# The MLP's turning and the gate moved behind the head loop of a one-token attention and MLP kernel

## The chip, the cores and the metric

The kernel runs on one core of a Trainium2 chip. The metric is the device time of one execution in microseconds. Three timed runs of the kernel before took 135.38, 135.53 and 135.91; the median is 135.53 us. One more execution was taken with the hardware profiler.

## What is computed

One token `x` of 576 features goes through two branches, mixed by a gate that is one number:

```python
g = sigmoid((x * gate_w).sum(-1))                       # gate_w: 576
q = (x @ wq) as 32 heads of 128                          # wq: 576 x 4096
k, v = the last 4096 of 32768 cached rows, 16 heads, each used by 2 query heads
p = softmax(q . k * 128 ** -0.5)
a = (p . v) @ wo                                         # wo: 4096 x 576
b = gelu_tanh(x @ w1 + b1) @ w2 + b2                     # w1: 576 x 4608, w2: 4608 x 576
out = g * a + (1 - g) * b                                # 1 x 576
```

All inputs are bf16. The cached rows in use are 33.6 MB of keys and values; the four weight matrices are 20 MB.

## The kernel before

**Transfers.** Keys and values come in four tiles each (`k_t`, `v_t`, 4 MB, 4 key heads a tile; here k0 to k3 and v0 to v3). They share three buffers of `kv_pool` with two tiles of w2. wq, w1 and wo come in two tiles each through two buffers of `w_pool`. Nearly all are issued by SP, in this order: the first part of wq, k0, `x9` (x as 64 rows of 9), the rest of wq, k1, two pieces of b1, k2, v0, first half of w1, k3, second half of w1, v1, v2, v3, two tiles of wo, and w2 in four groups, of which the last two are cut in pieces (L690). An issue that needs a buffer waits on SP until its last reader is done, and all later issues wait behind it: v0 takes k0's buffer, k3 that of k1, v1 that of k2, v2 that of v0, v3 that of k3, and so on. ScalarE issues five small transfers at the start: b2 in two halves, x as one row of 576 (`x_row`) in two halves, and the gate's weights (`gw_row`).

**Head of the program.** Constants are made on VectorE and GpSimd. Then x is spread over 128 partitions: TensorE makes `x_ps` from `x9` (L428) and four VectorE operations write `x2` (L436), which every product with wq and w1 uses as its stationary side. Then the gate: VectorE multiplies and sums `x_row` and `gw_row` (`junk`, `s0`, L440), TensorE spreads the sum to all partitions (`g_ps`, L445), ScalarE takes Exp (`ge`, L447), and VectorE makes `g_t` = g and `omg` = 1 - g (L448 to L452). Then come the transposes of the first four head units (L456), the query product (`q_ps`, L465), its turning (`qT`, `qz`) and the scores of three units.

**Transposes and scores.** A key tile is worked off in four units h (16 units in all). `transposes(h, i)`, i from 0 to 7, turns four 128 x 128 blocks by matmuls into one of three PSUM buffers (L281) and evicts them into `kT`, by VectorE for i = 0, 3, 6 (L290) and by ScalarE else (L292). `scores(h, s)` multiplies `kT` by the query (L311) into one PSUM tile for half of the units: units 0 to 7 are the first half, 8 to 15 the second.

**The head loop** (L618) goes over h from 3 to 15: it makes the transposes of unit h + 1, the scores of unit h, and between them, one function at a time, whatever stands in three lists. `chain` is the softmax of the first half (from h = 8): `row_max`, `turn_max`, `spread` (ScalarE's long Exp, L355) and four `put`, which turn the probabilities into `ez` (L366, L373). `tail` takes out the first value tile's sums. `mlp` is the MLP's middle, filled behind h = 13 once both halves of w1 are multiplied (`w1_mul`, L509): `take` adds b1 (`h_r`, L528), nine `turn_h` turn the features by two fp32 matmuls each (L539), and `act` makes gelu times `omg` out of them (L550 to L571, the result `gt`). Two of them are called for each i > 1, so they stand between the transposes of unit 15 in h = 14 and behind them. The first value tile's products (`values`, L397) run in h = 10 and 11.

**Behind the loop** (L659) `row_max`, `turn_max` and `spread` of the second half stand between the units of the second value tile (`unit(4)` to `unit(7)`); then `take` of `heads_out(1)` (`a_s`, L409 and L413), the four `put`, `norm`, and the units of the third and fourth value tiles. Then `ot`, `ow` (L696 to L712), the products with wo and three groups of w2 into `part` (L734), b2's part (`part_s`, L742), the last group of w2 in quarters into `y_ps` (L753), four copies into `y` (L769) and the output's transfer.

Each engine works off its instructions in the order of this text, since the order is written by hand (`manual_schedule`). One PSUM buffer (`ps_m`, one tag) serves all small products in turn: `x_ps`, `g_ps`, `qT`, `hT`, `mT`, `mb`, `pT`, `o_ps`, `t_ps`, `ow_ps`.

Of the kernel before, what the change touches and what calls it, by code (L numbers as in the profile page):

```python
# [8 lines left out]
FP32 = mybir.dt.float32  # L9
BF16 = mybir.dt.bfloat16  # L10
ACT = mybir.ActivationFunctionType
ALU = mybir.AluOpType
# [4 lines left out]
def kernel(  # L17
# [94 lines left out]
    def load_k(m):  # L112
        return load_kv(A_k_cache, m, "k_t")
# [14 lines left out]

    k_tiles, v_tiles = {}, {}

    x_row = const.tile([1, D], BF16, name="x_row")
    gw_row = const.tile([1, D], BF16, name="gw_row")

    b2_r = const.tile([P, D], BF16, name="b2_r")
    nc.gpsimd.memset(b2_r[:], 0.0)

    for o in (slice(0, D // 2), slice(D // 2, D)):
        nc.scalar.dma_start(out=b2_r[0:1, o], in_=B_b2.rearrange("(o n) -> o n", o=1)[:, o])
    for o in (slice(0, D // 2), slice(D // 2, D)):
        nc.scalar.dma_start(out=x_row[:, o], in_=A_x.rearrange("a b d -> (a b) d")[:, o])  # L140
    nc.scalar.dma_start(out=gw_row[:], in_=gate_w.rearrange("(o n) -> o n", o=1))

    x9 = const.tile([P // 2, NM], BF16, name="x9")

# [15 lines left out]
    for o in range(2):  # L160
        nc.sync.dma_start(
            out=b1_r[o : o + 32 * (NQ - 1) + 1 : 32],
            in_=B_b1.rearrange("(o t k n) -> o t k n", o=2, t=NQ, k=2)[o],
        )
    k_tiles[2] = load_k(2)


# [108 lines left out]
    def transposes(h, i):  # L276
        if i == 0:
            kT[h] = kT_pool.tile([P, W], BF16, name="kT", tag="kT")
        tp = ps_t.tile([P, BC * P], FP32, name="tp", tag="tp")
        for c in range(BC):  # L280
            nc.tensor.matmul(  # L281
                tp[:, c * P : (c + 1) * P],
                lhsT=k_tiles[h // UT][:, (h % UT) * NCH + i * BC + c, :],
                rhs=perm[:],
                start=True,
                stop=True,
            )
        dst = kT[h][:, i * BC * P : (i + 1) * BC * P]
        if i in (0, 3, 6):
            nc.vector.tensor_copy(out=dst, in_=tp[:])  # L290
        else:
            nc.scalar.copy(out=dst, in_=tp[:])  # L292
# [131 lines left out]

    x_ps = ps_m.tile([P, NM], FP32, name="x_ps", tag="m")
    nc.tensor.matmul(x_ps[:], lhsT=dup[:], rhs=x9[:], start=True, stop=True)  # L428
    ev, od = par[:, 0:1], par[:, 1:2]
    for dst, src, s in (  # L430
# [4 lines left out]
    ):  # L435
        nc.vector.tensor_scalar(out=dst, in0=src, scalar1=s, scalar2=None, op0=ALU.mult)  # L436

    junk = const.tile([1, D], BF16, name="junk")
    s0 = const.tile([1, 1], FP32, name="s0")
    nc.vector.tensor_tensor_reduce(  # L440
        out=junk[:], in0=x_row[:], in1=gw_row[:], scale=1.0, scalar=0.0,
        op0=ALU.mult, op1=ALU.add, accum_out=s0[:],
    )
    g_ps = ps_m.tile([P, 1], FP32, name="g_ps", tag="m")
    nc.tensor.matmul(g_ps[:], lhsT=ones_ff[0:1, :], rhs=s0[:], start=True, stop=True)  # L445
    ge = const.tile([P, 1], FP32, name="ge")
    nc.scalar.activation(out=ge[:], in_=g_ps[:], func=ACT.Exp, scale=-1.0)  # L447
    nc.vector.tensor_scalar(out=ge[:], in0=ge[:], scalar1=1.0, scalar2=None, op0=ALU.add)  # L448
    g_t = const.tile([P, 1], FP32, name="g_t")
    nc.vector.reciprocal(out=g_t[:], in_=ge[:])  # L450
    omg = const.tile([P, 1], FP32, name="omg")
    nc.vector.tensor_scalar(  # L452
        out=omg[:], in0=g_t[:], scalar1=-1.0, scalar2=1.0, op0=ALU.mult, op1=ALU.add
    )

    for h in range(UT):  # L456
        for i in range(NBL):
            transposes(h, i)
    v_tiles[0] = load_v(0)
# [59 lines left out]
    def gelu():  # L519

        NF = RJ * NG
        C0 = 0.7978845608028654
        h_r = small.tile([P, 2, 2, FB], FP32, name="h_r", tag="big")
        box = []

        def take():
            for k in range(2):
                nc.vector.tensor_tensor(  # L528
                    out=h_r[:, :, k, :],
                    in0=h_box[0][:, k : k + 1, 0:FB].to_broadcast([P, 2, FB]),  # L530
                    in1=b1_r[:, k : k + 1, :].to_broadcast([P, 2, FB]),
                    op=ALU.add,
                )
            box.append(ps_m.tile([P, RJ, 2, NG], FP32, name="hT", tag="m"))

        def turn_h(j):

            rows = h_r[:].rearrange("p e k n -> p (e k n)")
            nc.tensor.matmul(  # L539
                box[0][:, j, :, :].rearrange("p e g -> p (e g)"),  # L540
                lhsT=rows[:, j : j + RJ * (P - 1) + 1 : RJ],
                rhs=sel_f[:].rearrange("p e g -> p (e g)"),
                start=True,
                stop=True,
            )

        def act():
            hacc = const.tile([P, NF], FP32, name="hacc")
            h_v = hacc[:].rearrange("p (j g) -> p j g", j=RJ)
            nc.vector.tensor_scalar(  # L550
                out=h_v, in0=box[0][:, :, 0, :], scalar1=half[:, 0:1], scalar2=None, op0=ALU.mult
            )
            nc.vector.scalar_tensor_tensor(
                out=h_v, in0=box[0][:, :, 1, :], scalar=half[:, 1:2], in1=h_v, op0=ALU.mult,
                op1=ALU.add,
            )
            z2 = const.tile([P, NF], FP32, name="z2")
            nc.vector.tensor_tensor(out=z2[:], in0=hacc[:], in1=hacc[:], op=ALU.mult)
            poly = const.tile([P, NF], FP32, name="poly")
            nc.vector.tensor_scalar(  # L560
                out=poly[:], in0=z2[:], scalar1=2.0 * C0 * 0.044715, scalar2=2.0 * C0,
                op0=ALU.mult, op1=ALU.add,
            )
            u_t = const.tile([P, NF], FP32, name="u_t")
            nc.vector.tensor_tensor(out=u_t[:], in0=poly[:], in1=hacc[:], op=ALU.mult)
            e_t = const.tile([P, NF], FP32, name="e_t")
            nc.scalar.activation(out=e_t[:], in_=u_t[:], func=ACT.Exp, scale=-1.0)
            nc.vector.tensor_scalar(out=e_t[:], in0=e_t[:], scalar1=1.0, scalar2=None, op0=ALU.add)
            r_t = const.tile([P, NF], FP32, name="r_t")
            nc.vector.reciprocal(out=r_t[:], in_=e_t[:])  # L570
            nc.vector.scalar_tensor_tensor(  # L571
                out=gt[:].rearrange("p j g -> p (j g)"), in0=hacc[:], scalar=omg[:, 0:1], in1=r_t[:],
                op0=ALU.mult, op1=ALU.mult,
            )

        return [take] + [lambda j=j: turn_h(j) for j in range(RJ)] + [act]
# [37 lines left out]
        for s in range(2):  # L614
            scores(h, s)

    chain, tail, mlp = [], [], []
    for h in range(UT - 1, NU):  # L618
        if h == 2 * UT - 1:
            k_tiles[3] = load_k(3)  # L620
            w1_t.append(w1_load(1))
        if h == 3 * UT - 1:
            v_tiles[1] = load_v(1)
        for i in range(NBL):
            if h < NU - 1:
                transposes(h + 1, i)
            at = (4, 6) if h % (TB * UT) == 0 else (2, 5)
            if i in at:
                scores(h, at.index(i))
            if i in (0, 1, 3, 6, 7) and chain:  # L630
                chain.pop(0)()
            if i in (0, 5) and tail:
                tail.pop(0)()
            if i > 1 and mlp:
                for f in mlp[:2]:
                    f()
                mlp = mlp[2:]
            if h in (10, 11) and i % 2 == 1:
                for j in range(4):
                    n = (h - 10) * 16 + (i - 1) * 2 + j  # L640
                    values(n // NBL, n % NBL)
        if h == 11:
            tail = heads_out(0)
            w1_mul(0, w1_t[0])
        if h == 13:
            w1_mul(1, w1_t[1])
            mlp = gelu()
        if h == TB * UT - 1:
            chain = softmax(0)
    v_tiles[2] = load_v(2)  # L650
# [4 lines left out]
    def unit(h):  # L655
        for i in range(NBL):
            values(h, i)

    row_max()  # L659
    unit(UT)  # L660
    turn_max()
    unit(UT + 1)
    spread()
    unit(UT + 2)
    unit(UT + 3)
    take, turn_out = heads_out(1)
    take()
# [18 lines left out]
    for g in range(NG):  # L686
        if g % 3 == 0:
            t = kv_pool.tile([P, NCK * Dh], BF16, name="w2_t", tag="kv")
        at = (g % 3) * RJ * D
        cut = {NG - 2: (0, 5 * D), NG - 1: (0, 6 * D, 8 * D, RJ * D - DQ)}.get(g, (0,))  # L690
        for lo, hi in zip(cut, (*cut[1:], RJ * D)):
            nc.sync.dma_start(out=t[:, at + lo : at + hi], in_=w2_view[g, :, lo:hi])
        w2_t.append(t[:, at : at + RJ * D])
# [71 lines left out]

    y = const.tile([1, D], BF16, name="y")
    for t in range(NQ):
        copy = nc.scalar.copy if t < 2 else nc.vector.tensor_copy
        copy(out=y[:, quarters[t]], in_=y_ps[32 * t : 32 * t + 1, :])  # L769
    nc.sync.dma_start(out=out.rearrange("a b n -> (a b) n"), in_=y[:])  # L770

# [29 lines left out]
```

## Time and profile before

| | |
|---|---|
| median of 3 runs | 135.53 us (135.38 to 135.91) |
| the profiled execution's own time | 135.93 us |
| its span, first to last instruction | 134.1 us |
| its mean granted TensorE clock | 0.866 |
| busy: PE, PEld, DVE, ACT, POOL | 91.1, 59.4, 63.3, 50.3, 2.9 us |
| moved by DMA | 53.79 MB, 94.3% of 16 engines' span on SP's queue |
| chain that ended last | DMA 39%, PE 33%, DVE 15%, ACT 5%, issue 4% |

PE is TensorE's matmuls, PEld its weight loads, DVE VectorE, ACT ScalarE, POOL GpSimd. L281 is a line of the kernel. A row of the timeline gives start and busy time in us, engine, line, operation, tiles out and in, partitions by elements, how many were merged, and in brackets the idle time ahead of it and what ended it. The chain that ended last follows the work back from the last instruction. "Issue" is waiting that the profile doesn't explain. The granted clock is 1.0 when TensorE has full speed, 0.5 at half. The times in the text count from the span's start.

### The profile page before, as it was taken

To read this page: it belongs to the slowest core of one execution; us is meant where nothing else is said; L and a number is where in the kernel's file an instruction comes from. 1 tells how busy PE (TensorE), PEld (TensorE's weight loads), DVE (VectorE), ACT (ScalarE), POOL (GpSimd) and SP (SyncE) were. 2 spreads that over 40 slices of the span, in tenths; PEclk is the share of its full clock that TensorE was granted. 3 is DMA by queue.
4 is the path that set the end of the run, shared out by engine and by line. 5 is a ranking of instruction groups with operands and counts; after the bars stand their busy time and mean duration, and the time that the engine had idled before them with its cause. 6 is when DMAs were issued, how large, how long until landed. Compare 5 with 4: busy or idle time off the path is not lost.

```text
span 134.1 us, 2614 instructions
## 1 busy us (share of the span) xinstructions
PE 91.1 (68%) x1127; PEld 59.4 (44%) x1127; DVE 63.3 (47%) x138; ACT 50.3 (37%) x89; POOL 2.9 (2%) x10
## 2 busy tenths in 40 slices
PE   0000299886998885748989989599593585539842
PEld 0000189662666663536555756487122341125420
DVE  2940356673265557555544584624727434450021
ACT  0300057981387777573766467331050000000001
POOL 8000000000000000000000000000000000000000
PEclk9999999999999999995999999965555558965797
DMA  4998999899998998999989999998998999999950
GB/s 115 511 450 350 432 450 489 371 425 472 459 410 376 469 452 355 458 446 469 415 380 458 467 420 401 445 449 362 322 459 357 394 418 440 427 426 413 423 201 6
DMA packets 3431, 53.79 MB, mean 401 GB/s; under 512 B 590, under 2 KB 732, under 8 KB 1372
## 3 DMA queue, kind: packets, MB, share of 16 engines
q1 hardware_dynamic: 3410, 53.62, 94.3%
q8 instruction: 9, 0.15, 0.4%
q14 instruction: 2, 0.02, 0.0%
q10 hardware_dynamic: 10, 0.00, 0.0%
HBM read 53.62 MB, written 0.00 MB: 400 GB/s over the span
## 4 chain that ended last, share of the span: by engine, by line
DMA 39%; PE 33%; DVE 15%; ACT 5%; issue 4%; SPq 1%; DVEq 0%; ACTq 0%
DMA k_t<-in_A_k_cache_dram 16%; PE tp L281 14%; DMA w_t<-in_B_w_dram 14%; DMA x<-in_A_x_dram 9%; PE acc L397 6%; ACT kT L292 5%; DVE kT L290 5%; PE hT L539 3%; PE s_ps L311 2%; DVE ez L373 2%; PE h_ps L509 2%; DVE a_s L413 2%; PE q_ps L465 2%; PE pT L366 1%; DVE h_r L528 1%
## 5 line engine op out<-in xcount | busy, mean ns | idle before, releaser
L292 ACT CAST kT<-tp 128x512 bf16<-128x512 f32 x80 | 44.0, 587 | 30.6 <-PE tp L281 29.7
L281 PE MATMUL tp<-perm,k_t 128*128 128x128 bf16 x512 | 44.8, 234 | 4.3 <-DVE kT L290 2.1
L290 DVE CAST kT<-tp 128x512 bf16<-128x512 f32 x48 | 32.5, 689 | 30.3 <-PE tp L281 28.1
L281 PEld LDWEIGHTS <-k_t 128*128 128x128 bf16 x512 | 35.4, 107 | 15.2 <-issue 12.7
L311 PE MATMUL s_ps<-kT,qz 128*32 128x512 bf16 x128 | 12.8, 415 | 0.4 <-DVE qz L487 0.3
L397 PE MATMUL acc<-v_t,ez 128*32 128x512 bf16 x128 | 12.7, 506 | 0.0
L769 ACT CAST y<-y_ps 1x144 bf16<-1x144 f32 x2 | 0.5, 269 | 30.5 <-PE y_ps L753 30.5
L428 PE MATMUL x_ps<-x,dup 64*128 64x9 bf16 x1 | 0.2, 163 | 14.4 <-DMA x<-in_A_x_dram 14.4
L366 PE MATMUL pT<-pick,pr 128*128 128x128 bf16 x32 | 4.1, 271 | 5.6 <-DVE ez L373 4.2
L373 DVE TENSOR_TENSOR ez<-pT,own_r 128x512 bf16<-128x512 f32 x8 | 5.5, 688 | 4.1 <-PE pT L366 4.1
L366 PEld LDWEIGHTS <-pr 128*128 128x128 bf16 x32 | 2.9, 121 | 7.7 <-issue 5.1
L539 PE MATMUL hT<-sel_f,h_r 128*128 128x8 f32 x18 | 4.9, 378 | 1.4 <-DVE h_r L528 1.4
L355 ACT ACTIVATE pr<-ms,nb 128x2048 bf16<-128x2048 f32 x2 | 4.0, 2002 | 4.9 <-DVE nb L352 4.9
L445 PEld LDWEIGHTS g_ps<-s,ones_ff 1*128 1x128 f32 x2 | 0.5, 308 | 12.1 <-issue 12.1
L539 PEld LDWEIGHTS hT<-sel_f,h_r 128*128 128x128 f32 x18 | 4.7, 332 | 2.1 <-DVE h_r L528 1.7
L311 PEld LDWEIGHTS <-qz 128*32 128x32 bf16 x128 | 3.6, 95 | 4.0 <-issue 1.2
L397 PEld LDWEIGHTS <-ez 128*32 128x32 bf16 x128 | 3.6, 113 | 4.0 <-issue 2.6
L734 PE MATMUL part<-wo_t,ow 128*1 128x288 bf16 x64 | 4.0, 441 | 1.5 <-DVE ow L712 1.5
L447 ACT ACTIVATE ge<-g_ps 128x1 f32<-128x1 f32 x1 | 0.2, 172 | 12.0 <-PE g_ps L445 12.0
L742 DVE SCALAR_TENSOR_TENSOR part_s<-b_r,omg,part 128x576 f32<-128x576 bf16 x1 | 0.8, 814 | 8.2 <-PE part L734 8.2
L420 PE MATMUL o_ps<-m_r,a_s 128*128 128x8 f32 x8 | 1.8, 293 | 4.1 <-DVE a_s L413 3.2
L413 DVE SCALAR_TENSOR_TENSOR a_s<-acc,m_c,a_s 128x128 f32<-128x128 f32 x12 | 4.2, 351 | 0.4
(87 smaller groups left out, 52.8 us busy)
## 6 DMA issues: line engine op xcount, KB each, us to landing
k_t<-in_A_k_cache_dram SPq DMA_DIRECT2D x4, 4096.0 KB, 21.7
v_t<-in_A_v_cache_dram SPq DMA_DIRECT2D x4, 4096.0 KB
w_t<-in_B_w_dram SPq DMA_DIRECT2D x2, 2592.0 KB
wo_t<-in_A_wo_dram SPq DMA_DIRECT2D x2, 2304.0 KB
w_t<-in_B_w_dram SPq DMA_DIRECT2D x2, 1296.0 KB, 24.0
wq_t<-in_A_wq_dram SPq DMA_DIRECT2D x1, 2304.0 KB
wq_t<-in_A_wq_dram SPq DMA_DIRECT2D x1, 1792.0 KB, 14.0
w_t<-in_B_w_dram SPq DMA_DIRECT2D x1, 864.0 KB
```

What stands on the lines that cost most here:

```text
L281: nc.tensor.matmul(tp[:, c * P : (c + 1) * P], lhsT=k_tiles[h // UT][:, (h % UT) * NCH + i * BC + c, :], rhs=perm[:], start=True, stop=True,)
L290: nc.vector.tensor_copy(out=dst, in_=tp[:])
L292: nc.scalar.copy(out=dst, in_=tp[:])
L311: nc.tensor.matmul(s_tiles[t // TB][32 * g : 32 * (g + 1), :, :], lhsT=qz[:, HT * t + g, lo : lo + 32], rhs=kT_v[:, s * CB : (s + 1) * CB, ...
L355: nc.scalar.activation(out=pr[:].rearrange("p c i g -> p (c i) g"), in_=ms[:].rearrange("p c (i g) -> p (c i) g", g=1).to_broadcast([P, CB ...
L366: nc.tensor.matmul(pT[:, c, :, :].rearrange("p x r -> p (x r)"), lhsT=pr[:, n * BC + c, :, :].rearrange("p i g -> p (i g)"), rhs=pick[:].r ...
L373: nc.vector.tensor_tensor(out=ez[:, :, :, n, :, :].rearrange("p t b c r -> p c (t b) r"), in0=pT[:], in1=own_r[:].rearrange("p (a b r) -> ...
L397: nc.tensor.matmul(acc[t][32 * ct : 32 * ct + BC * R, :, :], lhsT=ez[:, t % TB, n // NN, n % NN, :, :].rearrange("p c r -> p (c r)"), rhs= ...
L413: nc.vector.scalar_tensor_tensor(out=a_s[:], in0=acc[t][:, c, :], scalar=m_c[:, c : c + 1], in1=a_s[:], op0=ALU.mult, op1=ALU.add,)
L465: nc.tensor.matmul(q_ps[32 * t : 32 * (t + 1), 0, 0:QC], lhsT=x2[:, m, :], rhs=wq_t[b // QP][:, off : off + QC], start=(m == 0), stop=(m = ...
L539: nc.tensor.matmul(box[0][:, j, :, :].rearrange("p e g -> p (e g)"), lhsT=rows[:, j : j + RJ * (P - 1) + 1 : RJ], rhs=sel_f[:].rearrange(" ...
L734: nc.tensor.matmul(part[32 * t : 32 * t + 1, k, 0:DB], lhsT=col, rhs=w[:, i * D + k * DB : i * D + (k + 1) * DB], start=(n == 0), stop=(n ...
```

## The change

x and the gate's weights are loaded as six rows of 96 each, by SP, between b1 and k2; ScalarE's three transfers for them go. The transposes of unit 0 come ahead of `x_ps` and `x2`. The whole gate (junk to omg) moves from there to behind the head loop, ahead of `row_max`. The MLP's middle leaves the loop: `take` comes behind `row_max`, the nine turnings and `act` behind `unit(6)`. In the last group of w2 the last cut moves from 144 to 288 columns before the end, and the four copies into `y` alternate between ScalarE and VectorE.

```diff
-    x_row = const.tile([1, D], BF16, name="x_row")
-    gw_row = const.tile([1, D], BF16, name="gw_row")
+    GR = 6
+    x_row = const.tile([GR, D // GR], BF16, name="x_row")
+    gw_row = const.tile([GR, D // GR], BF16, name="gw_row")
...
-    for o in (slice(0, D // 2), slice(D // 2, D)):
-        nc.scalar.dma_start(out=x_row[:, o], in_=A_x.rearrange("a b d -> (a b) d")[:, o])
-    nc.scalar.dma_start(out=gw_row[:], in_=gate_w.rearrange("(o n) -> o n", o=1))
...
+    nc.sync.dma_start(out=x_row[:], in_=A_x.rearrange("a b (r n) -> (a b r) n", r=GR))
+    nc.sync.dma_start(out=gw_row[:], in_=gate_w.rearrange("(r n) -> r n", r=GR))
     k_tiles[2] = load_k(2)
...
+    for i in range(NBL):
+        transposes(0, i)
+
     x_ps = ps_m.tile([P, NM], FP32, name="x_ps", tag="m")
...
-    junk = const.tile([1, D], BF16, name="junk")
-    s0 = const.tile([1, 1], FP32, name="s0")
...
-    omg = const.tile([P, 1], FP32, name="omg")
-    nc.vector.tensor_scalar(
-        out=omg[:], in0=g_t[:], scalar1=-1.0, scalar2=1.0, op0=ALU.mult, op1=ALU.add
-    )
-
-    for h in range(UT):
+    for h in range(1, UT):
         for i in range(NBL):
             transposes(h, i)
...
-    chain, tail, mlp = [], [], []
+    chain, tail = [], []
...
-            if i > 1 and mlp:
-                for f in mlp[:2]:
-                    f()
-                mlp = mlp[2:]
...
             w1_mul(1, w1_t[1])
-            mlp = gelu()
...
+    junk = const.tile([GR, D // GR], BF16, name="junk")
+    s0 = const.tile([GR, 1], FP32, name="s0")
+    nc.vector.tensor_tensor_reduce(
+        out=junk[:], in0=x_row[:], in1=gw_row[:], scale=1.0, scalar=0.0,
+        op0=ALU.mult, op1=ALU.add, accum_out=s0[:],
+    )
+    g_ps = ps_m.tile([P, 1], FP32, name="g_ps", tag="m")
+    nc.tensor.matmul(g_ps[:], lhsT=ones_ff[0:GR, :], rhs=s0[:], start=True, stop=True)
+    ge = const.tile([P, 1], FP32, name="ge")
+    nc.scalar.activation(out=ge[:], in_=g_ps[:], func=ACT.Exp, scale=-1.0)
+    nc.vector.tensor_scalar(out=ge[:], in0=ge[:], scalar1=1.0, scalar2=None, op0=ALU.add)
+    g_t = const.tile([P, 1], FP32, name="g_t")
+    nc.vector.reciprocal(out=g_t[:], in_=ge[:])
+    omg = const.tile([P, 1], FP32, name="omg")
+    nc.vector.tensor_scalar(
+        out=omg[:], in0=g_t[:], scalar1=-1.0, scalar2=1.0, op0=ALU.mult, op1=ALU.add
+    )
+
+    take_h, *turns, act = gelu()
     row_max()
+    take_h()
     unit(UT)
     turn_max()
     unit(UT + 1)
     spread()
     unit(UT + 2)
+    for f in turns:
+        f()
+    act()
     unit(UT + 3)
...
-        cut = {NG - 2: (0, 5 * D), NG - 1: (0, 6 * D, 8 * D, RJ * D - DQ)}.get(g, (0,))
+        cut = {NG - 2: (0, 5 * D), NG - 1: (0, 6 * D, 8 * D, RJ * D - DB)}.get(g, (0,))
...
-        copy = nc.scalar.copy if t < 2 else nc.vector.tensor_copy
+        copy = nc.scalar.copy if t % 2 == 0 else nc.vector.tensor_copy
```

More of the change, by code (lines that the diff above doesn't have):

```diff
@@ L436 @@
         nc.vector.tensor_scalar(out=dst, in0=src, scalar1=s, scalar2=None, op0=ALU.mult)
-    junk = const.tile([1, D], BF16, name="junk")
-    s0 = const.tile([1, 1], FP32, name="s0")
-    nc.vector.tensor_tensor_reduce(
-        out=junk[:], in0=x_row[:], in1=gw_row[:], scale=1.0, scalar=0.0,
-        op0=ALU.mult, op1=ALU.add, accum_out=s0[:],
-    )
[L444 to L450, printed above, removed]
-    omg = const.tile([P, 1], FP32, name="omg")
-    nc.vector.tensor_scalar(
-        out=omg[:], in0=g_t[:], scalar1=-1.0, scalar2=1.0, op0=ALU.mult, op1=ALU.add
-    )
-    for h in range(UT):
+    for h in range(1, UT):
         for i in range(NBL):
```

## The prediction

> **What bounds the kernel now.** I read the slices first, then busy time by stage, then SP's waits, then the chain of waits backwards from the end. The transfers are the floor: 53.79 MB go at 430 GB/s from 3 us to 128.5 us, and the row of DMA shares has no hole but a dent near its 28th digit. Busy time by stage (columns: window, its length, busy PE, PEld, DVE, ACT, POOL, granted clock, DMA share, GB/s) sizes that dent:
>
> ```profile
> 60.00:93.00 33.00, 29.55 (x368) 20.98 (x367) 16.53 (x29) 16.19 (x29) 0.00 (x0) 0.87 1.00 430
> 93.00:97.00 4.00, 2.55 (x20) 0.53 (x18) 3.05 (x10) 0.82 (x2) 0.00 (x0) 0.50 0.87 311
> ```
>
> Four microseconds at 311 instead of 430 GB/s lack 0.48 MB, 1.1 us of the stream. The reason is in SP's issues and the timeline:
>
> ```profile
> L104 SPq DMA_DIRECT2D v_t<-in_A_v_cache_dram x4: 534/538/575, 30.1 to 93.3; - x4
> 84.98 1.41 DVE L528 TENSOR_TENSOR h_r<-h_ps,b_r 128x576 f32<-128x576 f32 x2
> 92.68 0.59 PE L281 MATMUL tp<-perm,k_t 128*128 128x128 bf16 x4
> 93.20 1.36 PE L311 MATMUL s_ps<-kT,qz 128*32 128x512 bf16 x8
> 101.91 0.68 DVE L373 TENSOR_TENSOR ez<-pT,own_r 128x512 bf16<-128x512 f32 x1
> ```
>
> v3 is issued at 93.3, when the last transposes of k3 (PE, 92.68) free its buffer. The MLP's turning stands between those transposes (h_r from 84.98), and what was queued before v3 has run out by then. At the end PE waits for w2 pieces, and the chain's last transfer lands at 130.78:
>
> ```profile
> 126.67 0.53 PE L734 MATMUL part<-w_t,gt 128*1 128x288 bf16 x9 [0.24 <-DMA w_t<-in_B_w_dram]
> 128.08 0.54 PE L734 MATMUL part<-w_t,gt 128*1 128x288 bf16 x9 [0.88 <-DMA w_t<-in_B_w_dram]
> 130.13 1.42 PE L753 MATMUL y_ps<-w_t,gt 128*1 128x144 bf16 x36 [0.18 <-DMA w_t<-in_B_w_dram]
> 131.46 0.64 DVE L769 CAST y<-y_ps 1x144 bf16<-1x144 f32 x2 [1.98 <-PE y_ps L753]
> ```
>
> So the bound is DMA with compute close behind. How close: without waits the end would be L734 from 120.33 to 126.44 (wo, two w2 groups), 18 matmuls more at 64 ns (1.15), part_s 0.81, its row product 0.43, 36 matmuls at 15 ns (0.55), copies 0.64, and five hand-overs of 0.05: 130.1 instead of 132.1. **Compute has 2.0 us to lose.**
>
> **Head of the program.** x_ps, x2 and the gate go from before the first transposes. k0 is in at 14.1 (b1's issue, which waits for it, is at 14.12), so transposes start 2.6 us earlier than 16.68. The 32 groups take 13.3 us as now; the four x2 operations (0.62) fit in VectorE's idle time there. Query, q turning and 24 score matmuls (30.02 to 35.02) end at about 32.5. The next transposes need k1, and now start at 35.04 with PE just free, with k1 as releaser of PEld. k1's place in the stream is unchanged, so **the head gains nothing**; PE stands 2.5 us instead.
>
> That has a price: the granted clock.
>
> ```profile
> 57.47:60.88 3.41, 1.78 (x24) 1.55 (x25) 2.06 (x5) 1.90 (x5) 0.00 (x0) 0.96 1.11 476
> 60.88:64.30 3.42, 2.98 (x30) 2.08 (x28) 1.92 (x3) 1.40 (x3) 0.00 (x0) 0.54 0.93 402
> ```
>
> After a stretch of 3.41 us with PE busy 1.78 the clock was half for the next; after 84.78 to 88.19 (PE busy 2.01) again. In the changed head a stretch between 30 and 37 us holds the scores (1.55) and little else. At half clock twelve transposes take 1.32 (63.01) against 0.84 (44.34), a score group 0.62; a head with 32 and two groups is then 4.8 against 3.41 (40.00 to 43.41). A stretch of 3.41 loses 1.0; bounds 0 and 1.0, and as it may begin before k1 is there, I take **0.7**. The Trainium skill ("TensorE: Matmul & The Clock Gate", Part 1) lets the clock fall after an idle window of some 3.4 us; this gap is shorter, so by that rule nothing is lost here, which is the third rival below; the two stretches above, half busy and yet followed by half clock, speak against it.
>
> **ScalarE's table.** The gate's Exp is ScalarE's first, and the table load carries its line:
>
> ```profile
> 3.41 1.28 ACT L447 ACT_TABLE_LOAD   x1 [3.41 <-issue]
> 54.80 0.58 ACT L292 CAST kT<-tp 128x512 bf16<-128x512 f32 x1 [1.40 <-PE tp L281]
> 55.83 2.00 ACT L355 ACTIVATE pr<-ms,nb 128x2048 bf16<-128x2048 f32 x1 [0.45 <-DVE nb L352]
> ```
>
> Now it is free, at 3.41. With the gate behind the loop the first Exp is L355 of the first half. Evictions are CASTs, no load carries their line, so I expect it in ScalarE's queue after the eviction ending at 55.38: 55.38 + 1.28 = 56.66, and Exp starts 0.83 later, with hand-over **0.87**. Behind it wait three evictions, the pT matmuls and all later transposes. Bounds: 0 if the load stays ahead, 0.87 + 1.28 if the engine must also run empty for as long as the load's row. The Trainium skill ("ScalarE: Activation LUTs", What ACT_TABLE_LOAD costs) gives 1283 ns for the load, as here, and 1380 ns of draining more, which no row here shows; by it the sum below would be 1.4 higher.
>
> Both delays run on to h = 11, where PE now waits 0.38 for k3:
>
> ```profile
> 70.17 0.62 PE L281 MATMUL tp<-perm,k_t 128*128 128x128 bf16 x8 [0.38 <-DMA k_t<-in_A_k_cache_dram]
> ```
>
> Late there: 0.87 + 0.7 - 0.38 = **1.2 us**. Transfers don't see it: at 70 us w1 is still queued.
>
> **SP's queue.** Three ScalarE transfers go, two SP ones (six rows of 192 bytes) come before k2. SP's early issues wait for older landings (b1 for k0, 5.6 us). The new rows can wait no longer than for k0 and x9 (14.4), so k2's issue goes from 15.38 to about 16. The queue then holds wq and k1 until 33.5: nothing, and 0.6 us only if k2 had to wait for k1.
>
> **The loop's end.** Without the MLP, h = 14 runs like others: last transposes at 83.87 + 3.4 = 87.3, last eviction 87.9, scores end 88.35 against 94.56: **6.2 earlier**. v3 is issued at 87.4 + 1.2, long before the queue is empty: the dent closes and transfers end 1.1 sooner.
>
> **Behind the loop.** From the end of the scores to the first ez is 7.35 us now (94.56 to 101.91). The changed order puts in one line, by rows:
> - g_ps 0.55, then Exp to omg 0.74: 1.3 (six rows instead of one make junk shorter; it lies under the scores);
> - row_max 1.41 (95.19 to 96.60), behind the gate in VectorE's order;
> - take_h 1.42, ahead of turn_max's VectorE half;
> - m16 and m_all 0.55, mb to the next unit 0.85 (97.68 to 98.53), unit 6 0.95;
> - 18 turning matmuls, paced by their loads:
>
> ```profile
> L539 PEld LDWEIGHTS hT<-sel_f,h_r 128*128 128x128 f32 x18 | 4.7, 332 | 2.1 <-DVE h_r L528 1.7
> ```
>
>   4.7, not interleaved with transposes any more (four took 1.03 at full and 1.05 at half clock, so the clock doesn't matter);
> - act 2.44 (92.84 to 95.28), ahead of the four a_s operations (1.5), which now start while act would run.
>
> Sum 15.1; **7.8 more**. ScalarE's long Exp (2.0) and unit 7 lie beside it. Against 6.2 saved, ez and all that follows is 1.6 later, with the delay from h = 11 **2.8**.
>
> **The end.** 2.0 of it is the cover above, now that transfers come 1.1 sooner: 0.8 is left. One term is unknown: the third value tile ran at half clock, the fourth at full.
>
> ```profile
> 108.26 3.60 PE L397 MATMUL acc<-v_t,ez 128*32 128x512 bf16 x32
> 113.81 1.91 PE L397 MATMUL acc<-v_t,ez 128*32 128x512 bf16 x32
> ```
>
> The clock rose at 112.08, just after it. Moved against the clock's stretches it gains between 0 and 1.7; nearest to its own row, I take 0.3. The new cuts of the last group (72 and 72 KB for 108 and 36) and the copies shared differently save 0.3 only while transfers end last; when they don't, each engine still makes two copies: 0, bounds -0.3 and 0.
>
> Sum: 1.2 + 1.6 - 2.0 - 0.3 = +0.5. The profiled execution took 135.93 (span 134.1), 0.40 above the median 135.53; its own forecast is 136.4, the median's **136.0**.
>
> **Rivals.**
> 1. The third value tile gets the full clock: 1.4 more than I took, 134.6, faster. For it: the rise lay right behind it. Against: VectorE paces the ez before it, and PE is little busy there. Decides from 1.5 gained, from 0.8 if the clock also stays up after the head. Chance 0.18.
> 2. The table load holds ScalarE for twice its row at 55.4: +1.28, 137.3, slower. Place: before L355 in h = 8. It decides from 0.2 us on, since there is no cover left after 70.17. For it: nothing follows the load in the present trace to show when ScalarE is ready; against: only 1.28 is shown. Chance 0.22.
> 3. The clock stays up after the head: 0.7 less, 135.3. Chance 0.12.
> 4. My forecast, 0.48, its own range 135.3 to 136.8.
>
> That the change doesn't do what it says is no case: the moved lines must move.
>
> **How the numbers follow.** A measurement here tells 0.5%, 0.68 us, from no change. Faster: rival 1, 0.18. Same: rival 3 and 0.26 of the forecast, 0.38. Slower: rival 2 and the 0.22 of the forecast that lies above 136.2, 0.44. The range takes in most of rivals 1 and 2: 134.5 to 137.4.
>
> **What would show it.** Right: no dent behind 88 us, v3 issued by 89; first transposes near 14.1 and PE idle before 35; half clock in the stretch after; a table load at L355 near 55.4; PE's wait for k3 gone; gt done some 13 us behind the scores' end; no waits for w_t in L734, and ow near 123. Wrong: k2 issued after 33 us (then transfers have a new hole), the load still at 3.4, or PE still waiting for w2 pieces at the end, which would mean that compute wasn't late and the time is that of rival 1 or less.

## The result, and the profile after

The changed kernel took a median of 135.06 us (20 runs, 133.45 to 136.77) against 135.93 us (20 runs, 135.38 to 137.99) of the kernel before on the same chip: by the medians of all runs it is 0.6% faster. The ratio of the two is 0.988, 95% interval 0.985 to 0.991; ratios here leave out single runs over 1.5% above their kernel's fastest, 8 of the changed kernel's 20 and 2 of the other's. I had forecast 136.0, slower than before, and given "faster" 0.18. The profiled execution took 134.45 (span 132.7) for 135.93 (134.1).

By stage (columns as before: window, length, busy PE, PEld, DVE, ACT, POOL, granted clock, DMA share, GB/s):

```profile
60.00:93.00 33.00, 26.87 (x387) 17.20 (x386) 19.16 (x37) 17.12 (x32) 0.00 (x0) 0.99 1.00 428
93.00:97.00 4.00, 4.00 (x22) 3.15 (x22) 0.16 (x1) 2.09 (x2) 0.00 (x0) 0.50 0.99 426
```

The dent is closed: 426 for 311 GB/s. The timeline of the changed kernel shows the rest (start, busy time, engine, line, tiles, and the idle time ahead):

```profile
2.15 1.28 ACT L292 ACT_TABLE_LOAD   x1 [2.15 <-POOL ident masks.py:197]
35.22 0.84 PE L281 MATMUL tp<-perm,k_t 128*128 128x128 bf16 x12 [1.54 <-DMA k_t<-in_A_k_cache_dram]
70.59 0.62 PE L281 MATMUL tp<-perm,k_t 128*128 128x128 bf16 x8 [0.95 <-DMA k_t<-in_A_k_cache_dram]
87.42 0.53 SPq L104 DMA_DIRECT2D v_t<-in_A_v_cache_dram  x1
94.23 4.46 PE L524 MATMUL hT<-sel_f,h_r 128*128 128x8 f32 x18
102.47 0.68 DVE L373 TENSOR_TENSOR ez<-pT,own_r 128x512 bf16<-128x512 f32 x1
108.83 3.60 PE L397 MATMUL acc<-v_t,ez 128*32 128x512 bf16 x32
114.37 1.91 PE L397 MATMUL acc<-v_t,ez 128*32 128x512 bf16 x32
120.89 4.01 PE L737 MATMUL part<-wo_t,ow 128*1 128x288 bf16 x64 [1.50 <-DVE ow L715]
124.68 3.31 PE L737 MATMUL part<-w_t,gt 128*1 128x288 bf16 x54
129.14 0.75 PE L756 MATMUL y_ps<-w_t,gt 128*1 128x144 bf16 x36
129.94 0.64 DVE L772 CAST y<-y_ps 1x144 bf16<-1x144 f32 x2 [1.10 <-PE y_ps L756]
```

Read it from the end. The products into `part` and `y_ps` run through with no wait for a weight (L737, L756): compute ends last now, y is done at 130.58 (132.10 before), and the last transfer had landed at 129.17 (131.29 before). v3 is issued at 87.4 instead of 93.3. The price behind the loop is there too, but ez starts at 102.47, not the 104.7 that my sum gave, so ow (and with it L737) is 0.56 later than before, not 2.8. The table load stands at the first eviction (L292), at 2.15, where nothing waits. PE waits 1.54 for k1, where no wait showed before, and 0.95 for k3, where it waited 0.38.

### The profile page after: what moved, and what is told of

Same layout as the page of the kernel before. It is cut to its first block, busy times and chain, and to the rows that moved or that the text cites. A ratio compares the mean times of both kernels' runs of the same rounds, so it can differ in the third digit from the quotient of the medians.

```text
span 132.7 us, 2612 instructions
## 1 busy us (share of the span) xinstructions
PE 88.2 (66%) x1127; PEld 58.4 (44%) x1127; DVE 62.8 (47%) x138; ACT 50.2 (38%) x89; POOL 2.9 (2%) x10
## 4 chain that ended last, share of the span: by engine, by line
DMA 38%; PE 32%; DVE 17%; issue 6%; ACT 4%; SPq 2%; DVEq 0%; ACTq 0%
DMA k_t<-in_A_k_cache_dram 38%; PE tp L281 8%; PE acc L397 6%; PE part L737 5%; DVE kT L290 4%; PE hT L524 3%; DVE a_s L413 3%; ACT kT L292 3%; PE s_ps L311 2%; DVE ez L373 2%; PE h_ps L494 2%; PE pT L366 1%; PE o_ps L420 1%; SPq L126 1%; DVE h_r L513 1%
## 5 line engine op out<-in xcount | busy, mean ns | idle before, releaser
L292 ACT CAST kT<-tp 128x512 bf16<-128x512 f32 x80 | 43.9, 588 | 38.0 <-PE tp L281 36.9
L281 PE MATMUL tp<-perm,k_t 128*128 128x128 bf16 x512 | 43.4, 230 | 22.1 <-DMA k_t<-in_A_k_cache_dram 17.0
L281 PEld LDWEIGHTS <-k_t 128*128 128x128 bf16 x512 | 33.4, 103 | 33.6 <-DMA k_t<-in_A_k_cache_dram 17.8
L311 PE MATMUL s_ps<-kT,qz 128*32 128x512 bf16 x128 | 12.2, 395 | 0.6 <-DVE s L641 0.3
L397 PE MATMUL acc<-v_t,ez 128*32 128x512 bf16 x128 | 12.0, 475 | 0.0
L737 PE MATMUL part<-wo_t,ow 128*1 128x288 bf16 x64 | 4.0, 441 | 1.5 <-DVE ow L715 1.5
L420 PEld LDWEIGHTS o_ps<-m_r,a_s 128*128 128x128 f32 x8 | 1.4, 218 | 6.1 <-DVE a_s L413 5.1
L409 DVE TENSOR_SCALAR a_s<-acc,m_c 128x128 f32<-128x128 f32 x4 | 1.4, 347 | 4.2 <-PE acc L397 4.2
L737 PEld LDWEIGHTS <-ow 128*1 128x1 bf16 x64 | 2.0, 120 | 3.0 <-DVE ow L715 1.6
```

Source lines behind the costliest of these rows:

```text
L281: nc.tensor.matmul(tp[:, c * P : (c + 1) * P], lhsT=k_tiles[h // UT][:, (h % UT) * NCH + i * BC + c, :], rhs=perm[:], start=True, stop=True,)
L311: nc.tensor.matmul(s_tiles[t // TB][32 * g : 32 * (g + 1), :, :], lhsT=qz[:, HT * t + g, lo : lo + 32], rhs=kT_v[:, s * CB : (s + 1) * CB, ...
L397: nc.tensor.matmul(acc[t][32 * ct : 32 * ct + BC * R, :, :], lhsT=ez[:, t % TB, n // NN, n % NN, :, :].rearrange("p c r -> p (c r)"), rhs= ...
L420: nc.tensor.matmul(o_ps[:], lhsT=a_s[:], rhs=m_r[:], start=True, stop=True)
L737: nc.tensor.matmul(part[32 * t : 32 * t + 1, k, 0:DB], lhsT=col, rhs=w[:, i * D + k * DB : i * D + (k + 1) * DB], start=(n == 0), stop=(n ...
```

## The experiments

Ratios are against the kernel before, run on the same chip, with 95% intervals. Each kernel has six or twelve runs, table_again one. The kernel before had a median of 135.94 to 136.0 in all three sessions.

**again.** The changed kernel, for a second profile.

> The changed kernel itself, for its spread: its runs went from 133.45 to 136.77 us with mean granted clocks from 0.893 down to 0.847, the kernel before from 135.38 to 137.99. Theory A (compute ends last in the changed kernel, so that every half-clock stretch that falls on the chain lengthens it): times fall as the mean clock rises, about 0.8 to 1 us for each stretch of 3.41 us at half clock (0.013 of the mean clock), 133.4 to 136.8 again. Theory B (the spread is that of the transfers): times don't follow the clock, and the last landing moves with the time.

Measured: 135.3 us (133.6 to 136.31), ratio 0.987 (0.981 to 0.993). The profiled execution took 135.94. Its PE rows:

```profile
108.57 3.60 PE L397 MATMUL acc<-v_t,ez 128*32 128x512 bf16 x32
114.32 3.57 PE L397 MATMUL acc<-v_t,ez 128*32 128x512 bf16 x32
122.50 4.01 PE L737 MATMUL part<-wo_t,ow 128*1 128x288 bf16 x64 [1.50 <-DVE ow L715]
```

The fourth value tile took 3.57 for 1.91, at half clock. ow is 1.6 later for it and the execution 1.5 longer, while the last landing stays (128.89). The half clock over the value tiles ends at 117.73 here, at 112.94 in the first profile. The 26 runs go with the clock: at a mean granted clock of 0.889 to 0.893 the changed kernel took 133.45 to 133.71, at 0.858 to 0.860 134.22 to 135.53, at 0.847 to 0.848 135.88 to 136.77. That is Theory A: the spread of 3 us is that of the half clock, and by these two profiles it lies in where the long stretch ends. That was my unknown term at the third value tile; it reaches the fourth.

**mlp_only.** The kernel before with only the MLP's middle moved.

```diff
-    chain, tail, mlp = [], [], []
+    chain, tail = [], []
...
-            if i > 1 and mlp:
-                for f in mlp[:2]:
-                    f()
-                mlp = mlp[2:]
...
-            mlp = gelu()
...
+    take_h, *turns, act = gelu()
     row_max()
+    take_h()
     unit(UT)
...
     unit(UT + 2)
+    for f in turns:
+        f()
+    act()
     unit(UT + 3)
```

> The kernel before with only the MLP's middle moved: take_h behind row_max, turnings and act behind unit(6); head, gate, x rows, cuts and copies as before. Theory A (the whole gain is that v3 is issued some 5 us sooner, which closes the dent in the transfers, against the line that the MLP makes behind the loop): as fast as the changed kernel or a little faster, since the gate is out of the way behind the loop: 133 to 135, v3 issued by 89, last landing near 129. Theory B (the gain comes from the head, where transposes start 2.2 us sooner, and the MLP's move costs): 136 to 137.

Measured: 134.0 us (133.53 to 135.73), ratio 0.986 (0.982 to 0.991). The issue of v3 and the stage of the dent:

```profile
86.90 0.54 SPq L104 DMA_DIRECT2D v_t<-in_A_v_cache_dram  x1
93.00:97.00 4.00, 4.00 (x21) 3.95 (x24) 0.05 (x1) 0.98 (x2) 0.00 (x0) 0.50 0.91 393
```

The last landing is 129.03. This part alone carries the whole gain. In the other seven profiles with v3 issued by 88 this stage has 393 to 426 GB/s.

**head_only.** The kernel before with only the new loads and the new head; the gate stands between the first scores and the loop.

```diff
+    nc.sync.dma_start(out=x_row[:], in_=A_x.rearrange("a b (r n) -> (a b r) n", r=GR))
+    nc.sync.dma_start(out=gw_row[:], in_=gate_w.rearrange("(r n) -> r n", r=GR))
     k_tiles[2] = load_k(2)
...
+    for i in range(NBL):
+        transposes(0, i)
+
     x_ps = ps_m.tile([P, NM], FP32, name="x_ps", tag="m")
...
+    junk = const.tile([GR, D // GR], BF16, name="junk")
...
     chain, tail, mlp = [], [], []
```

> The kernel before with only the head changed: transposes of unit 0 first, x and gate weights in six rows by SP, and the gate between the first scores and the head loop; the MLP's middle stays in the loop. Theory A: k1's arrival near 35 takes back all that the head gains, so the time is that of the kernel before within 0.3 us, PE waits about 1.5 us for k1, the dent near 94 stays. Theory B (the head gives the gain): 1 to 1.5 us faster than before.

Measured: 136.37 us (135.95 to 137.65), ratio 1.004 (1.001 to 1.007). The head gains nothing; by itself it costs 0.4%.

**warm.** The changed kernel with six matmuls that nothing reads, where TensorE waits for k1.

```diff
+    warm = ps_m.tile([P, 512], FP32, name="warm", tag="m")
+    for _ in range(6):
+        nc.tensor.matmul(warm[:], lhsT=perm[:], rhs=kT[0][:, 0:512], start=True, stop=True)
     chain, tail = [], []
```

> The changed kernel with six idle 128x512 matmuls between the first scores and the head loop, where PE waits for k1 (results unused). Theory A with my rival on the clock (the wait before k1 costs the clock in some runs, and those are the long ones): runs above 135.3 us become rare, mean clock of the lowest runs rises above 0.855. Theory C (the half-clock stretches that matter come later, at the softmax of the first half and behind the loop): the same spread as the changed kernel, 133.4 to 136.8.

Measured: 134.83 us (133.74 to 136.39), ratio 0.992 (0.988 to 0.995). The spread stays, so idle time ahead of k1 isn't its cause. There was no clock loss behind the head to win back: the changed kernel's granted clock from 31.03 to 37.85 was 1.00.

**late_turns.** The changed kernel with the turnings between the four puts.

```diff
     row_max()
-    take_h()
...
     spread()
+    take_h()
     unit(UT + 2)
-    for f in turns:
-        f()
-    act()
     unit(UT + 3)
+    for f in turns[:2]:
+        f()
...
-    for f in puts:
+    for n, f in enumerate(puts):
         f()
+        for g in turns[2 * n + 2 : 2 * n + 4]:
+            g()
...
     sums_start()
+    act()
```

(`hT` moves to a buffer of `tp`, which is free by then.)

> The changed kernel with the turnings of the MLP features spread over the idle time of TensorE between the four puts, and their activation beside the third value tile, instead of between the softmax's Exp and the first put. Theory A (since the change the end is set by compute that is late behind the loop, and the transfers would let it end 1 us or more earlier): ez starts at about 95 us instead of 102.5, ow ends at 115 to 117 instead of 120.8, the last products wait for weights again, the last landing stays at 129.2, the vector y ends near 130.0 instead of 130.6, and above all the runs draw together, since a stretch of half clock over the value tiles no longer reaches the end: median 133.4 to 134.0, no run above 134.8, ratio to the kernel before 0.980 to 0.986. Theory B (the transfers alone set the end and the spread): ow is as early, the last landing moves with it or the time stays, median 134.8 to 135.3 and a spread of 3 us as in the changed kernel.

Measured: 133.84 us (133.66 to 134.12), ratio 0.982 (0.979 to 0.984). The six runs lie within 0.46 us. Its PE rows:

```profile
102.42 3.60 PE L397 MATMUL acc<-v_t,ez 128*32 128x512 bf16 x32
115.98 4.01 PE L739 MATMUL part<-wo_t,ow 128*1 128x288 bf16 x64 [1.50 <-DVE ow L717]
122.64 0.90 PE L739 MATMUL part<-w_t,gt 128*1 128x288 bf16 x18 [1.36 <-DMA w_t<-in_B_w_dram]
124.39 0.88 PE L739 MATMUL part<-w_t,gt 128*1 128x288 bf16 x9 [0.86 <-DMA w_t<-in_B_w_dram]
125.80 0.89 PE L739 MATMUL part<-w_t,gt 128*1 128x288 bf16 x9 [0.53 <-DMA w_t<-in_B_w_dram]
```

ow is done 4.9 us earlier, the waits for w2 are back, and the last landing is 128.94. Only 0.55 us of the 4.9 reach y (130.03), and 0.23 of them are the earlier landing. Theory A holds: the changed kernel's end was compute, and just below it lie the transfers. The runs no longer follow the clock: 133.66 and 133.80 at 0.836, 133.78 to 134.12 at 0.853 to 0.856.

**dent.** The changed kernel with v3 held back.

```diff
+    m_all_box = []
...
+        m_all_box[:] = [m_all]
...
     v_tiles[2] = load_v(2)
-    v_tiles[3] = load_v(3)
...
+    held = const.tile([1, P], FP32, name="held")
     turn_max()
+    nc.sync.dma_start(out=held[:], in_=m_all_box[0][:])
+    v_tiles[3] = load_v(3)
```

> The changed kernel with the load of v3 held back, by a small transfer ahead of it on its queue that reads m_all, to about 93 us, where the kernel before issued it; the order of the compute is untouched. Theory A (the earlier issue of v3 is what the change gains): the transfers fall again near 93 to 97 us, the last landing goes from 129.2 back to 131.0 to 131.5, ratio to the kernel before 0.997 to 1.004. Theory B (the transfers were not what ended last, or the dent was made up for by the queue behind it): last landing at most 129.9, ratio 0.985 to 0.991, as the changed kernel.

Measured: 136.15 us (134.94 to 137.94), ratio 1.000 (0.997 to 1.003). v3 was issued at 94.6, later than I wanted. The stage and the end of its profile:

```profile
93.00:97.00 4.00, 3.05 (x21) 2.18 (x17) 0.98 (x4) 2.10 (x2) 0.00 (x0) 0.54 0.63 213
```

```profile
130.81 0.55 PE L761 MATMUL y_ps<-w_t,gt 128*1 128x144 bf16 x24 [0.21 <-DMA w_t<-in_B_w_dram]
131.53 0.63 PE L761 MATMUL y_ps<-w_t,gt 128*1 128x144 bf16 x12 [0.17 <-DMA w_t<-in_B_w_dram]
```

The dent is back (213 GB/s), PE waits for w2 at the end, the last landing is 131.90, and the whole gain is gone. The landing is 0.4 later than I had expected, as v3 is. In this execution ow was also 1.23 later than in the changed kernel's, so the profile alone doesn't part the two. The runs do: where the clock was high they stayed long, 136.30 and 136.70 at 0.878 and 0.879, while the changed kernel took 134.12 and 134.45 at 0.884. All that differs is when v3, and the loads queued behind it, are issued.

**table.** The changed kernel with a second table load, where my prediction had put it.

```diff
+    tab = const.tile([P, 1], FP32, name="tab")
+    nc.scalar.activation(out=tab[:], in_=ones_ff[:, 0:1], func=ACT.Gelu)
```

> The changed kernel with one Gelu of 128x1 on ScalarE at the start, so that ScalarE's table is loaded there for Gelu and again for Exp at the softmax in the head loop, which is where my prediction put it. Theory A (the load there lies behind a wait for keys that the loop has anyway, 0.95 us at the thirteenth head): v3 is issued within 0.5 us of 87.4 and the time is the changed kernel's, ratio 0.985 to 0.991. Theory B (the step as predicted, 0.87 us or with the further hold of ScalarE 2.15 us, on the loop): v3 is issued at 88.3 to 89.6, compute at the end is that much later, time 0.9 to 2.2 us above the changed kernel, ratio 0.993 to 1.004.

Measured: 137.28 us (135.8 to 139.79), ratio 1.004 (1.000 to 1.008). Theory B. The profiled execution was the longest of the twelve, so the kernel was profiled a second time:

> The kernel of table once more, for a second profile, since the first one was one of the longest executions and had 13.7 us of half clock from 56.6 on. Theory A (the second table load costs what it holds ScalarE, 1.28 us, less the wait for k3): the load stands ahead of L355 again, Exp starts 0.6 to 0.9 us behind nb, the transposes of k3 start 0.3 to 1.5 us later than 70.59 and v3 is issued by 89. Theory B (the hold-up also draws out the half clock, as in the first profile): half clock for 6.8 us or more from 55 on, v3 issued at 89.5 or later.

Measured: 138.17 us, one run. Rows of PE, ACT and DVE:

```profile
34.89 1.46 PE L284 MATMUL tp<-perm,k_t 128*128 128x128 bf16 x12 [2.52 <-DMA k_t<-in_A_k_cache_dram]
```

```profile
56.31 0.58 ACT L295 CAST kT<-tp 128x512 bf16<-128x512 f32 x1 [2.03 <-PE tp L284]
56.91 1.28 ACT L358 ACT_TABLE_LOAD   x1
58.21 2.00 ACT L358 ACTIVATE pr<-ms,nb 128x2048 bf16<-128x2048 f32 x1
```

```profile
57.35 0.15 DVE L355 TENSOR_SCALAR nb<-mb 128x1 f32<-128x1 f32 x1
```

The load stands behind the eviction, as I had described it, and Exp starts 0.71 behind nb (57.50), where it is 0.03 in the changed kernel. It starts 0.02 behind the load's end: ScalarE isn't held longer than the load's row. k3's transposes start at 73.26, 2.7 later than in the changed kernel, which is more than the load: this execution also had half clock at 34.41 to 37.82 and for 13.65 us from 54.89 (3.41 in the changed kernel's). v3 is issued at 90.14 (90.82 in the first profile), later than the 89.6 that I had expected at most: Theory B of both expectations, and more than the load's own price. So the times don't tell what the load alone costs. All twelve runs of table had a mean clock of 0.848 or less, and the five at 0.847 to 0.848 took 135.80 to 136.77, no longer than the changed kernel's at that clock.

**fill.** The changed kernel with three matmuls that nothing reads behind each put.

```diff
+    fill = ps_t.tile([P, 512], FP32, name="fill", tag="tp")
     for f in puts:
         f()
+        for _ in range(3):
+            nc.tensor.matmul(fill[:], lhsT=perm[:], rhs=kT[NU - 1][:, 0:512], start=True, stop=True)
```

> The changed kernel with three 128x512 matmuls that nothing reads behind each of the four puts, where TensorE waits for VectorE. Theory A (the granted clock follows how busy TensorE was just before; the half clock over the third value tile and not its own work makes it 3.6 us): the stretch of half clock ends before 107 us, the third tile takes 1.9 to 2.2 us, ow ends 0.5 to 1.5 us earlier than 120.8 although the matmuls cost up to 0.6 us a put, and no run is above 135.3. Theory B (the half clock goes by other things): the third tile keeps 3.6 us, the matmuls hold up the puts by 0.6 us each, ow ends 1 to 2.5 us later, time 135.5 to 137.5.

Measured: 133.61 us (133.57 to 134.25), ratio 0.981 (0.979 to 0.984). PE rows:

```profile
106.72 1.06 PE L675 MATMUL fill<-kT,perm 128*128 128x512 bf16 x3
108.80 1.91 PE L397 MATMUL acc<-v_t,ez 128*32 128x512 bf16 x32
112.64 1.91 PE L397 MATMUL acc<-v_t,ez 128*32 128x512 bf16 x32
```

Doing more made it faster. The half clock ends at 107.21 (112.94 in the changed kernel's profile), during the last fills, which take 1.06 for 1.48, and the third value tile takes 1.91 for 3.60. The last two puts are held up by 0.3 each, and ow still comes 1.7 earlier, at 119.12. Theory A, with ow a little earlier than it said. The two profiles alone would not show that the matmuls did it. The stretch is 17.07 us long for 20.48, but it also began 2.3 earlier, ahead of them, and warm's, without them, is 17.07 too. The runs show it: all six had a mean clock of 0.877 to 0.894, the changed kernel's twenty 0.847 to 0.893.

**late_gate, late_cut, late_head.** Three neighbours of late_turns: with the gate ahead of the loop; with the old cut and copies; and with head, loads, gate, cut and copies as in the kernel before. The gate moves as in head_only; late_cut is this:

```diff
-        cut = {NG - 2: (0, 5 * D), NG - 1: (0, 6 * D, 8 * D, RJ * D - DB)}.get(g, (0,))
+        cut = {NG - 2: (0, 5 * D), NG - 1: (0, 6 * D, 8 * D, RJ * D - DQ)}.get(g, (0,))
...
-        copy = nc.scalar.copy if t % 2 == 0 else nc.vector.tensor_copy
+        copy = nc.scalar.copy if t < 2 else nc.vector.tensor_copy
```

> The kernel of late_turns with the gate taken out of the line behind the loop as well: it stands between the first scores and the loop, where TensorE waits for k1. Theory A (with the turnings out of the line, the transfers end last and compute has about 4 us to lose): ez and ow come 1.0 to 1.2 us earlier again (94.9 and 114.8), the last landing stays at 128.9 to 129.2 and the time is that of late_turns, 133.5 to 134.1, ratio 0.979 to 0.985. Theory B (the end still follows compute): the time falls by as much as ow, to 132.7 or 133.0.

> The kernel of late_turns with the last group's cut at 144 columns before its end and with the two copies of y by each engine side by side, both as in the kernel before. My prediction costs these edits at nothing while compute ends last and at 0.3 us for the new cut and copies once transfers end last, which they do here. Theory A (as costed): 0.2 to 0.4 us longer than late_turns, 134.0 to 134.3. Theory B (the last landing comes when the stream ends, however it is cut, and each engine makes two copies either way): within 0.15 us of late_turns.

> The kernel before with the MLP's middle behind the loop and its turnings between the puts, as in late_turns; head, loads, gate, cut and copies stay as before. Theory A (the head gains nothing, and its six-row transfers on SP's queue cost a little, 0.4% by head_only): 133.2 to 133.9, ratio 0.976 to 0.984, last landing 128.6 to 129.2. Theory B (the new head gains by earlier transposes once compute isn't what ends last): 0.4 us or more longer than late_turns, above 134.2.

Measured: late_gate 134.13 us, ratio 0.986 (0.982 to 0.990); late_cut 134.16, 0.986 (0.981 to 0.990); late_head 133.80 (133.70 to 133.87), 0.983 (0.979 to 0.988). In late_gate ow came at 114.85, 1.07 earlier than in late_turns, and the time didn't fall: compute no longer counts. late_cut is inconclusive. It is 0.32 above late_turns, but that ran in another session, and from the last landing to the end of y it took 1.06 (1.09 in late_turns), so the profile shows no gain by the new cut and copies; late_head has the old ones as well and took 133.80 beside it. late_head says that the change is no better for its new head: with the old one the six runs are as fast, within 0.17 us of each other.

## Why the prediction was wrong, step by step

The sum was +1.2 +1.6 -2.0 -0.3 = +0.5. With what the profiled execution measured, it is +0.1 +0.45 -2.0 +0 = -1.45; y came 1.52 earlier. So two terms were wrong by about 1.1 each, in the same direction: the delay at h = 11 (clock and table load), whose mechanism failed, and the line behind the loop, whose size did. The range of 134.5 to 137.4 held the median all the same, by its width.

- **The bound: right.** The dent came from v3's late issue, mlp_only takes it away and gains all, dent brings it back and loses all.
- **Transfers 1.1 us sooner: too small.** They ended 2.1 sooner. I had counted one window of 4 us. By GB/s from 93 to 105 the kernel before had 311, 385 and 397, the changed one 426, 442 and 404: 0.72 MB or 1.7 us at 430 GB/s, as the loss runs on, mainly into the second window (dent has 213, 393 and 393). The other 0.4 I can't place.
- **Compute has 2.0 us to lose: right.** 130.1 and the 0.56 by which ow was later make 130.66; y was done at 130.58.
- **The head gains nothing: right** (head_only). Its scores ended at 33.68, not 32.5.
- **Clock loss of 0.7 behind the head: the step that failed first.** PE waited 1.54 for k1, not 2.5, and kept the full clock. Where it did wait 2.52, in table_again, the stretch of half clock came, and twelve transposes took 1.46, for which I had 1.32 (in table's first profile the wait was 2.45, and it came too). The mechanism exists, the kernel doesn't get there: what failed is the wait, and with it the whole 0.7. Rival 3, at 0.12, had this. The Trainium skill ("TensorE: Matmul & The Clock Gate", Part 1) has a free-running window of 3413 ns and a fall after an idle one; the windows agree (stretches here are 3.41 us or multiples), the idle window doesn't: PE was busy for 1.37 us of the 3.41 ahead of that fall. Busy time alone doesn't sort the cases either: behind 31.03 to 34.44, with PE busy 1.81, the changed kernel kept its clock, and the kernel before lost it behind 84.53 to 87.94 with 2.01. (My first stretch was off the clock's steps by 0.24: from 57.23 to 60.64, where the granted clock is 1.00, PE was busy 1.54.)
- **The table load moves into the loop, 0.87: the step that failed outright.** I took it that evictions don't carry the load, because in the kernel before none did. There the gate's Exp came first on ScalarE. With the gate gone, the load went to the new first instruction, a CAST at L292, 2.15 us after the start. The load cost nothing. table shows what the step would have been worth at Exp if its place had been right, 0.68 us (0.71 for 0.03) of my 0.87; the kernel with it is as slow as before, but it also lost clock, and the runs don't part the two. My rival 2 asked whether ScalarE is held for twice the load's row; it is not (0.02 us). The Trainium skill's figure for draining ("ScalarE: Activation LUTs", What ACT_TABLE_LOAD costs) is not seen in either profile of table.
- **The loop's end 6.2 earlier: right**, 6.1 (88.46 for 94.56), and it is not delayed. Transposes of k3 do start 0.42 later, but because they wait 0.95 for k3.
- **15.1 us behind the loop: 1.1 too much**, the term that was mis-sized. It took 14.0. Up to the first turning I had added 6.5 in separate rows; they took 5.8, as rows overlap at their ends (h_r starts at 90.78, while mx ends at 90.87). The turnings took 4.46 for 4.7, and the first put's ez began 0.1 before the last a_s ended.
- **The third value tile's clock, 0.3:** nothing in this execution, 0.46 in warm's, 1.7 in fill's, and in again's the fourth tile lost 1.66. It isn't a term of one sign but the spread of the runs; rival 1 had it as a gain alone.

So the change helps by a margin that it nearly gives away. Its transfers end 2.1 sooner, and compute, now 0.56 later, lets 1.5 of that through. Where the half clock runs on to 117.7, it lets through almost nothing (135.94 in again).

Open: what keeps the clock low from 92 to 112 and when it rises (fill's runs show that more work on PE raises it, not the rule), and how much of table's 2 us is the load and how much the half clock that came with it.

## What to carry to other kernels

Work that can wait belongs behind whatever frees a buffer for the next load: the issue of v3, not the MLP, was worth the gain. What is moved should then go into an engine's gaps, not in one line; the same turnings between the puts gave 133.8 us with a spread of half a microsecond. And before pricing a load of ScalarE's table, ask which of its instructions comes first in the new order, whatever that is.

## What the runs showed of the hardware

- **Half clock comes in stretches of 3.41 us or multiples of it** (3.41, 6.83, 10.24, 13.65, 17.07, 20.48, 23.89), and being busy doesn't end it at once: in the changed kernel it began behind a stretch with PE busy 1.07 of 3.41 us (89.05 to 92.46), and PE was then busy for all of 93 to 97 at a granted clock of 0.50. Twelve added matmuls of 128x512 between the puts brought the mean clock to 0.877 to 0.894 in all six runs and made the kernel faster.
- **The table load goes to ScalarE's first instruction, be it a CAST** (2.15 at L292), and when a second is needed in the middle it takes 1.28 us, and the Exp behind it starts 0.02 after its end.
- **PE paused 0.78 us behind the first four groups of transposes** in all profiles with the new head but those of table (16.47 to 17.25 in the changed kernel), and in none with the old one. It is most of the reason why PE stood 1.54 and not 2.5 us ahead of k1. No run here tells the cause.
